# Seven block products instead of eight for chunk 7's second MLP product, in a kernel that already does so for chunks 8 to 11

## The chip, the cores and the metric

The kernel runs on one core of a Trainium2 chip. Its time is the device time of one execution in microseconds (us). A core has a matrix engine (TensorE, PE in the profile, with its weight loads as PEld), a vector engine (VectorE, DVE), an activation engine (ScalarE, ACT), a general engine (GpSimd, POOL) and a queue engine (SyncE, SP) that here only issues transfers. Each engine works through its own list of instructions in a fixed order and waits at an instruction until what it needs has been signalled.

## The reference

Four sequences of 768 positions with 8 heads of 64 go through an attention that sees 8 global and 96 local positions with a linear bias. Its output `x` (4 x 768 x 512) goes through a Fourier mixing layer and an MLP:

```
X = fft(fft(x, axis=1), axis=2)
u = x + real(X)
un = (u - mean(u)) / sqrt(var(u) + 1e-6)
out = u + max(un @ w_ch1, 0) @ w_ch2        # 512 -> 2048 -> 512
```

## The kernel before

**Stages.** The four batches b = 0..3 go through attention, then a two-stage Fourier transform by matrix products, then the MLP. The transform's first stage is in `y_unit` (matmuls at L979 into PSUM tiles `py`, four groups per batch, from sums `eA`, `ww` that VectorE makes at L832 to L859 and L936 to L953). The `py` groups are copied to `zy` on ACT (L994) or VectorE (L996), and POOL makes mirrored copies of them: `ww` (four copies, L1027) and `rev` (L1014 to L1016). The second stage is in `u_unit` (sixteen matmuls at L1059 into `pu`, one call for each pair of residues). VectorE adds the attention output to it (L1078, two instructions with a sum over the row, then L1082), which gives `u`; ACT and VectorE scale it to `un` (L1109, L1111), one half each.

**Chunks.** A chunk c is 256 rows of the MLP, two tiles t = 0, 1 of 128 rows; each batch has three, so c = 0..11, and batch 3 makes chunks 9, 10 and 11. From chunk 6 on `un` is transposed by a DMA that SP issues (L1133) into `unT`. The first product is eight units `ph(c, j)`, j = 0..7, each eight matmuls of 128x256 (L1180), evacuated with a relu to `hT` by ACT (L1186) or VectorE (L1187). ACT also squares `un` for the variance (L1118) once `unT` has landed, and POOL makes the reciprocal deviation (L1125, L1126).

**Second product, plain form (chunks 0 to 7).** `pg_unit` works in parts: for each tile t four parts of four matmuls of 128x512 (L1204), in one PSUM bank, 32 matmuls for the chunk. VectorE adds the scaled result to `u` (L1213), once for each tile, and SP stores the tile (L1218).

**Second product, seven-product form (chunks 8 to 11).** `CS = 8` selects it. The hidden dimension is cut into halves and the 512 output columns into halves, so the chunk's product is a 2x2 by 2x2 block product, and Winograd's scheme makes it from seven block products instead of eight. Each block product is eight matmuls of 128x256 (L1285). The sums that it needs of the weights, `w2_sums`, are made once by VectorE (L1239 to L1242, into the tiles `ex`, when the last attention is done). The sums of each chunk's blocks are four VectorE instructions in `s_sums`: s1 (L1258), s3 (L1261, in place in `hT`), s2 (L1264) and s4 (L1267); s1, s2, s4 go round four buffers in the mask tile `mk`. `pg_units` issues the products as P1 (tile `pgA`), P4 and P5 (`pgD`), P6 (`pgA` again), P3 and P2 (`pgD` again), P7 (`pgA` again). VectorE evacuates them at L1303 with five instructions: 256 columns after P1, 512 after P4 and P5, 256 after P6, 512 after P3 and P2, 512 after P7. The stores are at L1385. `pgA` and `pgD` take the two PSUM banks of the ring `pg`, the ones that the plain form uses too. The seven parts wait for each other: P6 for P1's evacuation (one bank), P3 and P2 for that of P4 and P5, P7 for that of P6.

**Order.** While the program is built, a planner (class `Plan`) decides the order of each engine's list. It keeps a model clock for each engine, takes the work that its costs say can start first, and looks up to ten units ahead in the Fourier and attention streams; the `ph` and `pg` streams are taken strictly in order, each from its head. Its costs are constants in the code, and a few loads have fixed landing times (`LAND`). So a changed unit changes the order of all that comes after it.

Of the kernel before, what the change touches and what calls it, by code (L numbers as in the profile page):

```python
# [181 lines left out]
def mm_us(n, k=1):  # L182
    return k * max(n / 2400.0 + 0.0025, 0.029)


def act(n):
    return 0.06 + n / 1200.0


def dve(n):  # L190
    return 0.085 + n / 960.0
# [11 lines left out]
def kernel(  # L203
# [68 lines left out]
    gb = np.zeros((64, 1))  # L272
# [15 lines left out]
    pl = Plan()  # L288
# [9 lines left out]
    def bank(tag, name, dtype=FP32):  # L298
        if tag in ("C", "D"):
            return early["pool"].tile([P, 2, 512 if dtype == FP32 else 1024], dtype, tag=tag, name=name, bufs=1)  # L300
        if tag == "xx":
            return ps.tile([P, 2, 512 if dtype == FP32 else 1024], dtype, tag=f"{tag}{tag.k}", name=name, bufs=1)
        if "late" not in early:
            early["ctx"].__exit__(None, None, None)
            early["late"] = ctx.enter_context(tc.tile_pool(name="psl", bufs=1, space=bass.MemoryType.PSUM))
        return early["late"].tile([P, 512], FP32, tag=f"{tag}{tag.k}", name=name, bufs=1)
# [5 lines left out]
    def free(tag, i):  # L312
        i -= NBUF[tag]
        return [("free", tag, i)] if i >= 0 else []

    def buf(tag, i, shape, dtype, users):
        pl.users(("free", tag, i), users)
        return wk.tile(shape, dtype, tag=f"{tag}_{i % NBUF[tag]}", name=f"{tag}_{i}", bufs=1)
# [183 lines left out]
    def BANKS(b):  # L502
        return ("xx", "C", "D") if b < 2 else ("xx",)

    def CD(b, ring):
        if b == 1 and ring in ("C", "D"):
            pl.left[("CD",)][0] += 1
            return [("CD",)]
        return [("CD",)] if b == 0 else []

    def RA(b):
        return 2 if b else 0
# [190 lines left out]
    def glob(b, halves):  # L703

        ns = [HP * b + 2 * half + i for half in halves for i in range(2)]
        needs = [("qkT", n) for n in ns] + [("kG", n, s) for n in ns for s in range(2)]

        def run(start, ring):
            pg = bank(ring, f"pgl_{b}_{halves[0]}")
            for half in halves:  # L710
                for i in range(2):
                    hp = 2 * half + i
                    if b >= FB:
                        for x in range(2):
                            nc.tensor.matmul(pg[32 * half:32 * half + 32, 0, x * 256:(x + 1) * 256].rearrange("p (a t m) -> p a t m", a=2, t=2),
                                             kG[b % 2][:, hp, :],
                                             TT[HP * b + hp][:, 0].rearrange("p (i t a m) -> p i a t m", t=2, a=2, m=64)[:, x + 1],
                                             start=(i == 0), stop=(i == 1), tile_position=(0, 32 * half), skip_group_check=True)
                        continue
                    nc.tensor.matmul(pg[32 * half:32 * half + 32, 0, :], kG[b % 2][:, hp, :],  # L720
                                     TT[HP * b + hp][:, 0, 256:S], start=(i == 0), stop=(i == 1),
                                     tile_position=(0, 32 * half))
            e = pl.pe(mm_us(512, 2 * len(halves)), start, True)
            for half in halves:
                pl.tok[("gldone", b, half)] = e
            for n in ns:
                pl.used(("free", "qkT", n), e)
            rows = slice(32 * halves[0], 32 * halves[-1] + 32)

            def ex():  # L730
                if ("free", "eg", b) not in pl.left:
                    pl.users(("free", "eg", b), 8)
                A(EG[rows], pg[rows, 0, :], AF.Exp, gb_sb[rows], 0.125)
            pl.later([("ACT", act(512), ex)], free("eg", b), e, [("eg", b, half) for half in halves], CD(b, ring), ring=ring, rank=RA(b))
        ATT.append((needs, BANKS(b), run))

    X = {}
# [432 lines left out]
    def ph_unit(c, jp):  # L1170
        needs = [("unT", c), ("w1", jp // 2)] + (free("hT", 4 + c) if jp == 0 else []) + [("CD",)]

        def run(start, ring):
            if jp == 0:
                HT[c] = buf("hT", 4 + c, [P, NJ, CH], FP16, 2 if c < CS else 1)
            ph = bank(ring, f"ph_{c}_{jp}")
# [45 lines left out]

    NK = NJ // 2
    HC = Dm // 2
    CS = 8
    SX = {}

    def W2T(i):
# [16 lines left out]
    def s_sums(c):  # L1245
# [5 lines left out]
        def new(i):  # L1251
            k = 3 * (c - CS) + i
            pl.users(("free", "sx", k), 2 if i < 2 else 1)
            SX[c, i] = mk.rearrange("p h n -> p (h n)")[:, (k % 4) * NK * P:(k % 4 + 1) * NK * P].rearrange("p (k n) -> p k n", n=P)
            return SX[c, i]
# [14 lines left out]
        def sfree(i):  # L1270
            k = 3 * (c - CS) + i - 4
            return [("free", "sx", k)] if k >= 0 else []
        pl.later([("DVE", us, s1)], hs + sfree(0), 0.0, [("s", c, 1)], rank=1)
        pl.later([("DVE", us, s2)], [("s", c, 1)] + sfree(1), 0.0, [("s", c, 2)], [("free", "sx", 3 * (c - CS))], rank=1)
        pl.later([("DVE", us, s4)], [("s", c, 2)] + sfree(2), 0.0, [("s", c, 4)], [("free", "sx", 3 * (c - CS) + 1)], rank=1)
        pl.later([("DVE", us, s3)], [("s", c, 1)], 0.0, [("s", c, 3)], rank=1)

    def pg_units(c):
# [23 lines left out]
        def stt(o, x, t, acc):  # L1302
            V.scalar_tensor_tensor(o, x, r(t), acc, op0=ALU.mult, op1=ALU.add)  # L1303
# [9 lines left out]
        def p45(start, ring):  # L1313
# [4 lines left out]
            e = pl.pe(2 * one_us, start)  # L1318
            pl.used(("free", "sx", 3 * (c - CS)), e)
            pl.later([("DVE", dve(Dm), lambda: stt(u(1), D_, 1, u(1)))],  # L1320
# [273 lines left out]
```

## Time and profile before

| | |
|---|---|
| four runs before | 264.11, 265.17, 265.50, 267.08 us; median 265.34 |
| the profiled execution | 264.11 us, its span 262.3 us |
| TensorE matmuls | 244.4 us busy, 93% of the span |
| VectorE | 176.6 us, 67% |
| ScalarE | 146.4 us, 56% |
| GpSimd | 67.9 us, 26% |
| TensorE clock granted | 1.00 |

A row's start is given from the span's start. The durations of matmuls overlap, since they are pipelined, so what a unit costs TensorE is read from the starts of consecutive units: eight matmuls of 128x256 start 0.87 us before the next unit, four of 128x512 start 0.86 us before it. The same holds for VectorE, whose rows overlap a little: a 128x512 addition at L1213 lasts 0.74 us and the next instruction starts 0.66 us after it.

### The profile page before, as it was taken

The page shows a single profiled execution, that of the slowest core. Times are in us where ns is not written, and L with a number is a line of the kernel's source. Part 1 is how long each engine was busy: PE and PEld are TensorE (multiplying, and loading weights), DVE is VectorE, ACT ScalarE, POOL GpSimd, SP SyncE. Part 2 cuts the span into 40 slices and gives each one's busy share as a digit, 9 for nine tenths or more (in the row PEclk, how much of TensorE's full clock was granted, in tenths as well). Part 3 has the DMA queues.
Part 4 walks back from the last instruction along what each step waited for, and adds up shares of the span by engine and source line. Part 5 has one row for each costly group of instructions (what it writes and reads, how often), then busy time and mean ns, then how long its engine had stood idle before and what let it go on. Part 6 is the DMA issues. An engine that isn't in the chain of part 4 may idle for free.

```text
span 262.3 us, 7311 instructions
## 1 busy us (share of the span) xinstructions
PE 244.4 (93%) x3080; PEld 178.7 (68%) x3080; DVE 176.6 (67%) x360; ACT 146.4 (56%) x249; POOL 67.9 (26%) x133
## 2 busy tenths in 40 slices
PE   8787668599999999999999999999999999999994
PEld 2565555487856876774685565679677568888883
DVE  4568997842599746661398968777998734644463
ACT  1468879776476577963861445995346165433300
POOL 1445398652030515123110523011001320010000
PEclk9999999999999999999999999999999999999999
DMA  7999969999599993995999895502071330310222
GB/s 216 296 292 302 308 173 248 217 215 207 117 260 241 250 195 96 222 223 102 237 157 207 240 234 115 140 0 42 17 202 65 82 84 36 82 42 2 80 81 82
DMA packets 76386, 42.02 MB, mean 160 GB/s; under 512 B 33474, under 2 KB 72514, under 8 KB 76354
## 3 DMA queue, kind: packets, MB, share of 16 engines
q1 hardware_dynamic: 69298, 32.65, 55.7%
q0 software_dynamic: 4224, 4.19, 9.5%
q10 hardware_dynamic: 2832, 4.72, 6.5%
q8 instruction: 24, 0.39, 0.6%
q14 instruction: 8, 0.07, 0.1%
HBM read 31.59 MB, written 9.44 MB: 156 GB/s over the span
## 4 chain that ended last, share of the span: by engine, by line
PE 79%; ACT 6%; DVE 4%; POOL 4%; DMA 3%; issue 2%; SPq 1%; POOLq 0%; ACTq 0%; DVEq 0%
PE ph L1180 31%; PE pg L1204 21%; PE pgD L1285 5%; PE pgA L1285 4%; PE pav L768 4%; PE py L979 3%; PE pu L1059 3%; DMA u<-in_v_dram 3%; PE sc L630 2%; ACT ex L657 2%; POOL ww L1027 2%; PE pav L757 2%; SPq L399 1%; DVE qkT L586 1%; DVE x L788 1%
## 5 line engine op out<-in xcount | busy, mean ns | idle before, releaser
L1180 PE MATMUL ph<-unT,w 128*128 128x256 f16 x768 | 93.3, 273 | 0.0
L1180 PEld LDWEIGHTS <-w 128*128 128x128 f16 x768 | 72.8, 98 | 13.6 <-issue 2.6
L1186 ACT ACTIVATE hT<-ph 128x512 f16<-128x512 f32 x78 | 46.1, 597 | 45.1 <-PE ph L1180 43.3
L1204 PE MATMUL pg<-w,hT 128*128 128x512 f16 x256 | 60.0, 379 | 0.0
L1204 PEld LDWEIGHTS <-hT 128*128 128x128 f16 x256 | 24.3, 98 | 24.6 <-issue 0.7
L657 ACT ACTIVATE ex<-sc 128x992 f16<-128x992 f32 (+2 forms) x24 | 20.6, 928 | 7.4 <-PE sc L633 7.3
L654 ACT ACTIVATE er<-sc 128x992 f16<-128x992 f32 (+2 forms) x24 | 21.6, 928 | 4.5 <-PE sc L630 4.3
L1213 DVE SCALAR_TENSOR_TENSOR u<-pg,sm,u 128x512 f32<-128x512 f32 x16 | 11.9, 745 | 12.9 <-PE pg L1204 12.8
L669 DVE TENSOR_TENSOR ex<-er,mk 128x992 f16<-128x992 f16 (+2 forms) x24 | 15.4, 643 | 7.1 <-ACT er L654 6.8
L1027 POOL COPY ww<-zy 128x512 f16<-128x512 f16 x16 | 10.0, 650 | 29.9 <-PE py L979 29.9
L1125 POOL TENSOR_SCALAR sm<-sm 128x2 f32<-128x2 f32 x12 | 2.5, 209 | 56.9 <-ACT un L1118 54.6
L768 PEld LDWEIGHTS <-ex 128*128 128x128 f16 x352 | 15.1, 97 | 2.7 <-issue 1.8
L768 PE MATMUL pav<-v,ex 128*128 128x65 f16 x352 | 16.3, 193 | 0.5 <-ACT ex L657 0.3
L1118 ACT ACTIVATE un<-un 128x512 f16<-128x512 f16 x24 | 14.9, 627 | 3.0 <-DMA unT<-un 2.5
L1187 DVE TENSOR_SCALAR hT<-ph 128x512 f16<-128x512 f32 x18 | 12.4, 687 | 6.1 <-PE ph L1180 5.9
L403 ACT ACTIVATE qk<-qs 128x768 f16<-128x768 f32 x11 | 9.2, 841 | 12.1 <-DMA out_dram<-u 7.2
L1109 ACT ACTIVATE un<-u,sm 128x512 f16<-128x512 f32 x16 | 11.2, 718 | 8.2 <-DVE sm L1082 8.2
L1078 DVE SCALAR_TENSOR_TENSOR u<-pu,xr 128x512 f32<-128x512 f32 x18 | 11.7, 686 | 4.0 <-PE pu L1059 3.8
L493 POOL CAST v<-qs 128x768 f16<-128x768 f32 x8 | 6.6, 829 | 27.4 <-DMA qs<-in_v_dram 27.4
L1285 PEld LDWEIGHTS <-hT 128*128 128x128 f16 x128 | 12.5, 98 | 1.6
L788 DVE TENSOR_TENSOR x<-pav,rc 128x512 f16<-128x512 f32 (+1 forms) x21 | 12.9, 615 | 0.7
L536 POOL COPY kG<-qkT 64x8 f16<-64x8 f16 x32 | 9.8, 307 | 13.3 <-DVE qkT L586 10.1
(122 smaller groups left out, 377.3 us busy)
## 6 DMA issues: line engine op xcount, KB each, us to landing
out_dram<-u SPq DMA_DIRECT2D x23, 256.0 KB, 2.4
w<-in_moe_w_ch_dram POOLq DMA_DIRECT2D x8, 512.0 KB, 19.3
qs<-in_q_dram SPq DMA_DIRECT2D x9, 384.0 KB, 5.6
qs<-in_k_dram SPq DMA_DIRECT2D x9, 384.0 KB, 5.3
qs<-in_v_dram SPq DMA_DIRECT2D x16, 192.0 KB, 5.2
xr<-xd ACTq DMA_DIRECT2D x3, 768.0 KB, 5.7
u<-in_v_dram SPq DMA_DIRECT2D x5, 384.0 KB, 7.2
w<-in_q_dram SPq DMA_DIRECT2D x4, 384.0 KB, 6.3
```

The source lines that it names most:

```text
L654: A(mine(), cut(pa), AF.Exp, 0.0, 0.125)
L657: A(cut(expst[hp][:, :, g * 512:g * 512 + (384 if g == 2 else 512)]), cut(pa), AF.Exp, 0.0, 0.125)
L669: VT(o, mine(), m, op=ALU.mult)
L768: nc.tensor.matmul(po[:, jj, hh * 65:(hh + 1) * 65], lhsT, v16[b % 2][:, i, h, 0:65], start=(jp == 0 and a == 0), stop=(a == len(ops) - 1) ...
L788: VT(X[b][:, 2 * jp:2 * jp + 2, first * Dh:(first + nh) * Dh].rearrange("p j (h d) -> p j h d", d=Dh), pv[:, :, :, 0:Dh], rc.to_broadcast( ...
L1027: nc.gpsimd.tensor_copy(rev[:, n], T[("y", b)][:, n, :, :, ::-1])
L1118: A(x, x, AF.Square, accum_out=MV[c][:, a, 2:3])
L1180: nc.tensor.matmul(ph[:, a * CH:(a + 1) * CH].rearrange("p (x m) -> p x m", x=2), W1[0][:, d, jb * P:(jb + 1) * P], UNT[c][:, :, d, :], st ...
L1186: pl.later([("ACT", act(512), lambda: A(dst, ph, AF.Relu)), ("DVE", dve(512), lambda: V.tensor_scalar_max(dst, ph, 0.0))], [], e, [("h", c ...
L1187: ("DVE", dve(512), lambda: V.tensor_scalar_max(dst, ph, 0.0))],
L1204: nc.tensor.matmul(pg, HT[c][:, jb, t * P:(t + 1) * P], W2[0][:, jb, :], start=(jb == 0), stop=(jb == NJ - 1))
L1285: nc.tensor.matmul(o, lhs(j), rhs(j), start=(first and j == 0), stop=(j == NK - 1), skip_group_check=True)
```

## The change

`CS` goes from 8 to 7, so chunk 7 takes the seven-product form too. The second line changed adds a need to the global keys' exponential (L733), that the small bias tile `gb` has been loaded; the order up to chunk 6 is the same with it as without.

```diff
@@ glob
-            pl.later([("ACT", act(512), ex)], free("eg", b), e, [("eg", b, half) for half in halves], CD(b, ring), ring=ring, rank=RA(b))
+            pl.later([("ACT", act(512), ex)], free("eg", b) + [("c", "gb")], e, [("eg", b, half) for half in halves], CD(b, ring), ring=ring, rank=RA(b))
@@
     NK = NJ // 2
     HC = Dm // 2
-    CS = 8
+    CS = 7
     SX = {}
```

For chunk 7, 32 matmuls of 128x512 become 56 of 128x256; two VectorE additions of 512 columns become five (three of 512, two of 256 columns); VectorE gets four sums of 1024 elements per partition. The first difference in any list lies in the first product of chunk 8. TensorE's list from there, with `6.t` for the parts of chunk 6's tile 1:

```
before: 6.t part 0 | ph 8.3 8.4 | 6.t part 1 | ph 8.5 8.6 | py0 py3 | ph 8.7 | 6.t part 2 |
        py1 py2 | 6.t part 3 | pu 9 | 7 part 0 | pu 11 | 7 part 1 | pu 10 | 7 parts 2 to 6 |
        ph 9.0 9.1 | 7 part 7 | ph 9.2 9.3 | 8 P1 | ph 9.4 9.5 | 8 P4 P5 | ph 9.6 9.7 | 8 P6 |
        ph 10.0 10.1 | 8 P3 P2 | ...
        ph 11.6 11.7 | 10 all seven | 11 all seven
after:  6.t part 0 | ph 8.3 8.4 | 6.t part 1 | ph 8.5 8.6 | 6.t part 2 | ph 8.7 | 6.t part 3 |
        py0 py3 | 7 P1 P4 P5 | py1 py2 | 7 P6 | pu 9 | 7 P3 P2 | pu 10 | pu 11 | 7 P7 |
        8 P1 P4 P5 P6 | ph 9.0 9.1 | 8 P3 P2 | ph 9.2 9.3 | 8 P7 | ph 9.4 9.5 | 9 P1 | ...
        ph 11.6 11.7 | 10 P3 P2 P7 | 11 all seven
```

VectorE's list in the same place (F is the transform's first sums, L851 to L859, G the second, L936 to L953):

```
before: F, G | py3 copy | relu 8.7 | sums s1 s2 s3 s4 of 8 | 6.t add | pu 9 add, un | pu 10 add, un |
        7 add | 7 add | ...
after:  s1 of 7 | first of F | s2 of 7 | relu 8.3 | s3 of 7 | rest of F | s4 of 7 | G | 6.t add |
        s1 of 8 | 7 P1 add | s3 of 8 | 7 P4 P5 add | s2 of 8 | py2 copy (1024) | 7 P6 add | s4 of 8 |
        pu 9 add | 7 P3 P2 add | un 9 | pu 10 add | 7 P7 add | un 10 | 8 P1 add | ...
```

ACT copies py0, py3 and py1 instead of py0, py1 and py2. On SP the store of chunk 7's tile 0 now stands ahead of the transpose for chunk 9, and that of its tile 1 ahead of the transpose for chunk 10; before, both stood behind the two transposes.

## The prediction

> **What bounds the kernel now.** I read the busy time by stretch first, then TensorE's timeline over the stage that changes, then VectorE's and the transposes. By stretches (columns: length, then busy us and instructions of TensorE's matmuls, weight loads, VectorE, ScalarE, GpSimd, then the clock and DMA share):
>
> ```profile
> 192.15:211.87 19.72, 19.34 (x158) 13.24 (x156) 15.68 (x35) 8.24 (x13) 3.73 (x7) 1.00 0.35 101
> 211.87:244.17 32.30, 32.30 (x293) 28.58 (x292) 14.59 (x26) 15.37 (x31) 2.64 (x6) 1.00 0.18 55
> ```
>
> The new order begins near 192.15 and chunk 9's first product near 211.87. TensorE is full in both stretches; VectorE is at 80% in the first, where it also makes batch 3's transform, and at 45% in the second. So matmul time counts one for one, as long as VectorE and the transposes keep up. TensorE's timeline:
>
> ```profile
> 201.73 1.03 PE L1204 MATMUL pg<-w,hT 128*128 128x512 f16 x4
> 202.59 1.06 PE L1059 MATMUL pu<-t,zy 128*128 128x128 f16 x16
> 203.48 1.03 PE L1204 MATMUL pg<-w,hT 128*128 128x512 f16 x4
> 204.35 0.28 PE L1059 MATMUL pu<-t,ww 128*128 128x128 f16 x2
> 205.00 0.96 PE L1059 MATMUL pu<-t,ww 128*128 128x128 f16 x14 [0.38 <-POOL ww L1027]
> ...
> 207.55 4.48 PE L1204 MATMUL pg<-w,hT 128*128 128x512 f16 x20
> 211.87 1.91 PE L1180 MATMUL ph<-unT,w 128*128 128x256 f16 x16
> ...
> 222.34 1.04 PE L1285 MATMUL pgA<-ex,mk 128*128 128x256 f16 x8
> 223.21 1.91 PE L1180 MATMUL ph<-unT,w 128*128 128x256 f16 x16
> ```
>
> The starts give the unit prices: 20 wide matmuls take 211.87 - 207.55 = 4.32, so 0.216 each; eight narrow ones take 223.21 - 222.34 = 0.87 (0.8735 over many). The only stall is 0.54, before 205.00 (204.35 + 0.11 for two matmuls = 204.46), for the mirrored copies.
>
> **The product itself.** 32 x 0.216 = 6.91 goes; 56 x 0.1092 = 6.11 comes: **-0.80 us**. Chunks 8 to 11 already run at this narrow price, and a weight load lasts 98 ns against 109 ns from one narrow matmul to the next, so the loads stay hidden, narrowly.
>
> The Trainium skill, "TensorE: Matmul & The Clock Gate", section "Back-to-back issue gap", speaks against the change: in streams of a weight load and a matmul it gives about 131 ns for each 512-column matmul and 81 ns for a 128-column one. An estimate between these for 256 columns is 98 ns, and by it the change would cost 56 x 0.098 - 32 x 0.131 = +1.3 us. The rows here, 216 and 109 ns, contradict it and follow that section's formula for isolated matmuls instead, so the measurement decides.
>
> **VectorE's added work.** A sum of 1024 elements takes 0.61 to the next start (0.73 where it needs the one before it):
>
> ```profile
> 201.06 0.69 DVE L1264 TENSOR_TENSOR mk<-mk,hT 128x1024 f16<-128x1024 f16 x1
> 201.67 0.68 DVE L1261 TENSOR_TENSOR hT<-hT 128x1024 f16<-128x1024 f16 x1
> 202.27 1.10 DVE L1267 TENSOR_TENSOR mk<-hT,mk 128x1024 f16<-128x1024 f16 x1
> 203.29 0.74 DVE L1213 SCALAR_TENSOR_TENSOR u<-pg,sm,u 128x512 f32<-128x512 f32 x1
> ```
>
> Four sums: 2.44. Evacuations: 3 x 0.66 + 2 x 0.40 instead of 2 x 0.66: +1.46. Together +3.9 on VectorE, none of it on TensorE; it is hidden if nothing that TensorE needs comes late. So I walk the new order with these intervals.
>
> *First sums.* All four of chunk 7's sums and the relu of 8.3 now stand ahead of G. F and G as a block move by 4 x 0.61 + 0.61 = 3.05. In the trace the sums that py0 needs end about 196.5, now near 199.5. TensorE does 6.t's last two parts and ph 8.7 first: 197.37 + 2 x 0.865 + 0.873 = 199.97. Margin 0.47, no stall; without it each further 0.1 on VectorE costs 0.1. The relu of 8.3 ends by 195.1, ph 8.5 starts at 195.62. G ends at 201.2, py1 starts at 203.75.
>
> *7 P1 to pu 9.* py0 and py3 end at 201.06, P1 at 201.93; P4 needs the bank that the 6.t addition frees at 202.0 (stall 0.07), P5 ends at 203.75, py2 at 205.28, P6 at 206.15, pu 9 at 207.04. P6 needs VectorE's addition of P1, done by 202.9.
>
> *Mirrors.* In the trace POOL starts them 0.29 after py2, takes 2.88 for `ww` and 0.84 for `rev`, so 205.57 to 209.3. 7 P3 and P2 end at 208.79; pu 10 then needs `rev` and waits some 0.15 after two matmuls; pu 11 ends at 210.72. The old stall of 0.54 goes in exchange: **-0.4**.
>
> *Back-pressure.* VectorE copies py2 (1024 wide, about 1.15) from 205.5, adds P6, makes s4 of chunk 8, then pu 9's 1.33 and 0.20, P3 and P2, `un`, pu 10, and only then P7, whose bank 8 P4 needs. I get P7's addition ending at 212.5, 8 P4 starting at 212.55 instead of 212.47 (+0.1), 8 P6 ending at 215.2.
>
> In the fence above L1267 took 1.10 instead of 0.68 while POOL copied (202.02 to 204.95); s3, which only its last 0.3 shares with the copies, stayed at 0.68. In the new order s4 of chunk 8 lies wholly beside the copies too. So all that follows on VectorE may come 0.42 later, and 8 P4 with it. The ends are 0.1 and 0.55; I take **+0.55**, since L1267's is the same instruction beside the same copies. 8 P6 then ends at 215.6.
>
> The Trainium skill, "SBUF — State Buffer", section "Who interferes with whom", says that a VectorE instruction with two SBUF inputs and a GpSimd one that reads SBUF exclude each other for a whole instruction, whichever began first. By that rule s4 waits for a whole copy (0.72) at worst, and the sum would be 0.3 worse than with the 0.42.
>
> *The transpose.* Before, `un` of chunk 9 was done at 206.2 and TensorE reached it at 211.87:
>
> ```profile
> 205.48 0.72 ACT L1109 ACTIVATE un<-u,sm 128x512 f16<-128x512 f32 x1 [2.27 <-DVE sm L1082]
> 210.91 0.63 ACT L1118 ACTIVATE un<-un 128x512 f16<-128x512 f16 x1 [0.83 <-DMA unT<-un]
> ```
>
> The view of chunk transposes gives:
>
> ```profile
> DMA to landing us min/median/max: 3.0/3.1/4.8
> ```
>
> The transposes started at 206.2 and 222.6 took 4.7 and 4.8, those at 164.7 and 210.1 took 3.1. Now `un` is done at 210.25 to 210.75 (VectorE: pu 9 at 207.65 or 208.1, statistics 1.53, P3 and P2 0.67, half of `un` 0.45). The store ahead of it on SP waits for P3 and P2's addition, just earlier, and takes 0.33 to issue. So the transpose starts at 210.4 to 210.9, lands at 213.5 at best and 215.2 to 215.7 at worst. TensorE wants it at 215.2, or 215.6 if VectorE is late, which moves both. I take no stall. The cover is 0 to 2 us; once gone, each us is a us.
>
> *Behind it.* ACT's scaling of chunk 11 waits for VectorE's pu 11 addition (216.2 to 217.7, after chunk 7's second store, issued about 213 and landed in 2.0 to 2.4), and behind it stand chunk 10's squares and relu 9.2. They end by 219.9, relu 9.2 is due at 220.1; hidden. Chunk 10's transpose starts near 213.4 and is wanted after 222. From 8 P3 on 48 units of 0.8735 remain: 41.93. The tail keeps about 0.4 of waits between blocks: before, three of 0.14; now 0.28 where 11 P1 waits for the bank of 10 P3 and P2, whose addition stands behind two sums, and 0.14 where 11 P3 waits. So TensorE ends at 215.6 + 41.9 + 0.4 = 257.9 (257.5 from the other end), against 258.54 before: **-0.6**, at best -1.0. (By terms: -0.80, -0.4 at the mirrors, +0.55, +0.07, the same tail.) After it come the same addition and store.
>
> The profiled execution took 264.11 (span 262.3), the fastest of four; the median is 265.34. -0.6 on the execution gives 263.5, on the median **264.7**, which I forecast. 1% (2.65 us) is about what a measurement here can tell from no change; the forecast lies inside it.
>
> **Rivals.** *Gain eaten on VectorE.* py0 comes 0.2 late and the mirrored copies 0.4 (four of them took 2.27 at 155.67 and 2.94 at 202.02, beside the sums): -0.6 + 0.6 = 0, **265.3**. For it: VectorE has hardly a gap from 190 to 213 in the walk. Against: 0.47 of margin at py0.
>
> *Slower: chunk 9's transpose comes late.* Place: ph 9.0. Chunk 7's store (256 KB) goes out 0.4 before the transpose; if the transpose waits until it has landed, that is 210.0 + 2.0 to 2.4 = 212.3, and with 4.8 it lands at 217.1, or 217.5 with VectorE late, 1.9 after TensorE is ready: -0.6 + 1.9 = +1.3, **266.6**. It decides from a landing 0.6 after that point, at 216.2. For it: nothing is left on TensorE's list to fill with, where before 20 wide matmuls stood. Against: the transpose's 3.1 at 164.7 came 1.9 after a store, with a transpose between them.
>
> *No saving by itself:* if narrow matmuls with chunk 7's operands ran at more than 123 ns, the product would gain nothing: -0.6 + 0.8, **265.5**. Every narrow row speaks against it.
>
> **How the numbers follow.** Forecast (gain of 0.3 to 1.0, 264.3 to 265.0) 0.60; eaten on VectorE 0.20; late transpose 0.16; no saving 0.04. The range reaches from the forecast's best, 264.3, less 0.7 for scatter (the lowest run stood 1.2 under the median), 263.6, to the late transpose with a little of VectorE's on top, 266.8. Chances: faster by over 1% 0.03, only by scatter; within 1% 0.90; slower by over 1% 0.07, the late transpose with more than the 1.9.
>
> **What would show it.** Chunk 7's seven products at 0.87 each; no wait of `py` on VectorE; one short wait of `pu` on `rev`; a wait at 8 P4 of 0.1 to 0.55; no idle before ph 9.0; TensorE's last unit near 257.7. I am wrong if TensorE idles before ph 9.0, at py0, or if a relu comes late after chunk 11's scaling on ACT.

## The result, and the profile after

| | before | changed |
|---|---|---|
| median of the timed runs | 265.27 us (79 runs) | 263.97 us (53 runs) |
| ratio, 95% interval | | 0.9954 [0.9941, 0.9968] |
| the profiled execution, its span | 264.11, 262.3 us | 263.23, 261.4 us |

The changed kernel is faster by 1.2 us (0.8 to 1.6). The forecast was 0.6 us faster, 264.7 us. So the time lies inside the range and within 1% of before, with the forecast's sign, and the gain is twice the one forecast. It is also more than the 0.3 to 1.0 that the forecast allowed itself: 263.97 lies below its 264.3 to 265.0, in the part of the range that was added for scatter, so that the range held is partly luck. The ratio compares the means of the executions without the few that were slower as a whole, so it is not quite the ratio of the two medians.

The busy times on the changed kernel's page, section 1 (busy us, share of the span, instructions):

```profile
PE 243.2 (93%) x3104; PEld 181.0 (69%) x3104; DVE 178.7 (68%) x366; ACT 146.5 (56%) x250; POOL 66.8 (26%) x133
```

TensorE lost 1.2 of its 244.4 us and VectorE gained 2.1, less than the 3.9 of added work, in part because one relu went over to ACT (17 at L1187 where there were 18). The changed kernel by stretches, with the columns of the prediction's first fence; the first runs from the new order's start to chunk 9's first product:

```profile
192.45:215.31 22.86, 22.86 (x219) 19.11 (x217) 20.90 (x45) 8.30 (x14) 3.63 (x8) 1.00 0.39 114
215.31:250.00 34.69, 34.69 (x320) 31.11 (x318) 15.14 (x28) 16.78 (x32) 2.54 (x6) 1.00 0.14 41
```

TensorE shows no idle time in the first stretch, where before it lacked 0.38 of 19.72. VectorE is at 20.90 of 22.86, 91% where it was 80%, and back at 44% in the second. TensorE's timeline of the changed kernel (start, duration, instruction, count, idle time before and its releaser):

```profile
199.41 1.03 PE L1204 MATMUL pg<-w,hT 128*128 128x512 f16 x4
200.27 1.26 PE L979 MATMUL py<-t,ww 128*128 128x256 f16 x10
201.36 1.04 PE L1285 MATMUL pgA<-w,hT 128*128 128x256 f16 x8
202.24 1.04 PE L1285 MATMUL pgD<-ex,hT 128*128 128x256 f16 x8
...
209.02 0.28 PE L1059 MATMUL pu<-t,zy 128*128 128x128 f16 x2
209.13 0.28 PE L1059 MATMUL pu<-t,rev 128*128 128x128 f16 x2
...
211.68 1.04 PE L1285 MATMUL pgA<-w,hT 128*128 128x256 f16 x8
212.69 1.03 PE L1285 MATMUL pgD<-ex,hT 128*128 128x256 f16 x8
...
214.43 1.04 PE L1285 MATMUL pgA<-ex,mk 128*128 128x256 f16 x8
215.31 0.93 PE L1180 MATMUL ph<-unT,w 128*128 128x256 f16 x7
```

Chunk 7's blocks follow each other in 0.87 (201.36, 202.24), and py0 comes straight behind the last wide part (199.41 + 0.86 = 200.27). No row carries a bracket with idle time: a wait under about 0.17 hides in the modelled ends and shows only in the starts. There is one, before 8 P4: 211.68 + 0.87 = 212.55, and it starts at 212.69, 0.14 late. Chunk 9's first product follows 8 P6 at once (214.43 + 0.87 = 215.30). The tail of the same view holds the two others:

```profile
250.24 1.04 PE L1285 MATMUL pgA<-ex,hT 128*128 128x256 f16 x8
251.46 1.03 PE L1285 MATMUL pgA<-w,hT 128*128 128x256 f16 x8 [0.18 <-DVE u L1303]
...
254.07 1.04 PE L1285 MATMUL pgA<-ex,mk 128*128 128x256 f16 x8
255.08 1.03 PE L1285 MATMUL pgD<-w,mk 128*128 128x256 f16 x8
```

11 P1 waits 0.35 (251.46 - 250.24 - 0.87) and 11 P3 waits 0.14. TensorE's last unit is issued by 257.69, where it was 258.54.

**Where the time went.** From the start of chunk 6's tile 1 (192.15 before, 192.45 after; all that differs lies behind it) to the end of the last unit TensorE took 66.39 us before and takes 65.24, so **-1.15**, which agrees with the 1.2 of the clock. (The execution's own difference is only 0.88 because the changed one reached this point 0.30 later.) The terms:

| term of the prediction | forecast | measured |
|---|---|---|
| the product of chunk 7 | -0.80 | -0.80 |
| the mirrors (0.54 before pu 11, then pu 10) | -0.4 (0.15 stays) | -0.54 (nothing stays) |
| stall at 7 P4 | +0.07 | 0 |
| back-pressure, 8 P4 | +0.55 | +0.14 |
| tail | 0 | +0.08 (0.49 instead of 0.41) |
| sum | -0.6 | -1.12 |

The rest of the document asks whether these terms are causes or a lucky sum, and why two were mis-sized. Below, "TensorE's stretch" is always this one, from that start to the end of the last unit. It tells 0.1 us (the changed kernel gave the same to a hundredth in each of three traces), which the clock cannot: its intervals reach 0.7 to 0.9 us to either side in the experiments. All kernels below have the second changed line too, and the kernel before has not. With chunk 7 in the plain form three of them differ from it by -0.42, +0.61 and -0.56 us on the clock and by -0.40, +0.71 and -0.56 in TensorE's stretch, so that line by itself costs or saves nothing that shows.

### The profile page after: what moved, and what is told of

Read it like the earlier page. It is cut to its first block, busy times and chain, and to the rows that moved or that the text cites. A ratio compares the mean times of both kernels' runs of the same rounds, so it can differ in the third digit from the quotient of the medians.

```text
span 261.4 us, 7364 instructions
## 1 busy us (share of the span) xinstructions
PE 243.2 (93%) x3104; PEld 181.0 (69%) x3104; DVE 178.7 (68%) x366; ACT 146.5 (56%) x250; POOL 66.8 (26%) x133
## 4 chain that ended last, share of the span: by engine, by line
PE 66%; DMA 17%; DVE 7%; ACT 4%; issue 2%; SPq 2%; POOL 1%; POOLq 0%; ACTq 0%
PE ph L1180 25%; PE pg L1204 15%; DMA w<-in_moe_w_ch_dram 9%; PE pgD L1285 6%; PE pgA L1285 5%; PE pu L1059 3%; PE py L979 3%; DMA u<-in_v_dram 3%; PE sc L630 2%; PE pav L768 2%; DMA qs<-in_k_dram 2%; DVE x L788 2%; DMA xr<-xd 2%; SPq L399 2%; DMA xd<-hT 2%
## 5 line engine op out<-in xcount | busy, mean ns | idle before, releaser
L1186 ACT ACTIVATE hT<-ph 128x512 f16<-128x512 f32 x79 | 46.8, 598 | 48.6 <-PE ph L1180 48.5
L1204 PE MATMUL pg<-w,hT 128*128 128x512 f16 x224 | 52.5, 379 | 0.0
L1213 DVE SCALAR_TENSOR_TENSOR u<-pg,sm,u 128x512 f32<-128x512 f32 x14 | 10.4, 744 | 8.7 <-PE pg L1204 8.7
L1187 DVE TENSOR_SCALAR hT<-ph 128x512 f16<-128x512 f32 x17 | 11.7, 687 | 5.8 <-PE ph L1180 5.7
L1303 DVE SCALAR_TENSOR_TENSOR u<-pgD,sm,u 128x512 f32<-128x512 f32 (+1 forms) x11 | 7.7, 701 | 10.0 <-PE pgD L1285 9.8
```

Of the source, the lines that this page charges most:

```text
L1186: pl.later([("ACT", act(512), lambda: A(dst, ph, AF.Relu)), ("DVE", dve(512), lambda: V.tensor_scalar_max(dst, ph, 0.0))], [], e, [("h", c ...
L1187: ("DVE", dve(512), lambda: V.tensor_scalar_max(dst, ph, 0.0))],
L1204: nc.tensor.matmul(pg, HT[c][:, jb, t * P:(t + 1) * P], W2[0][:, jb, :], start=(jb == 0), stop=(jb == NJ - 1))
```

## The experiments

**The changed kernel again.** Theory A is the sum of terms: the product's 0.80 and the mirrors' wait are both real. Theory B is that the product gains nothing by itself and that the whole gain is the new order's, the wait that went. The run repeats the changed kernel on another chip.

> The changed kernel again, as the yardstick for the other runs on this chip. Theory A (the gain is a sum of separate terms on TensorE: -0.80 for chunk 7's cheaper product, -0.54 for the wait before pu 11 that goes, +0.14 and +0.08 for new waits at 8 P4 and in the tail): -1.1 us, a ratio near 0.996. Theory B (narrow products save nothing here, the gain is only the wait that went and the rest is scatter): -0.4 to -0.5, a ratio near 0.998.

264.83 against 266.11, ratio 0.9957 [0.9928, 0.9985]. TensorE's stretch is 65.24 again, with the waits 0.13, 0.35 and 0.13 in the same places. The gain exceeds B's 0.4 in the trace, and the terms are the same to a hundredth.

**Only pu 10 and pu 11 exchanged, chunk 7 in the plain form.** In batch 3 pu 11 has to stand behind pu 10, as it does in the changed kernel.

```diff
+            pl.tok[("puo", b, pr)] = e
-        MIX.append((needs + [("c", "t2")], BANKS(b), run))
+        MIX.append((needs + [("c", "t2")] + ([("puo", b, 1)] if b == B - 1 and pr == 2 else []), BANKS(b), run))
-    CS = 7
+    CS = 8
```

> CS stays 8, so chunk 7 is in the plain form, but batch 3's second transform is held to the order pu 9, pu 10, pu 11, as in the changed kernel: the one part of the new order that took the 0.54 us wait away. Theory A: TensorE does 7 part 0 and 1 between pu 9 and pu 10 (1.73 us), so pu 10 waits for the mirrored copies only 0.1 to 0.2 us: -0.4 us, ratio 0.9985. Theory B: nearly all of the changed kernel's gain, -1 us, ratio 0.996.

265.32, ratio 0.9984 [0.9951, 1.0017]. TensorE's stretch is 65.99, 0.40 less than before: the 0.54 goes and pu 10 waits 0.15. That is the prediction's term at the mirrors, alone and to the hundredth. It leaves 0.75 for the product and its waits, so B falls. But in the changed kernel pu 10 did not wait, while the four copies took as long here as before (2.94, then 2.93), so something else also differs.

**The seven-product form from chunk 9 on.** One chunk fewer in it than before.

```diff
-    CS = 7
+    CS = 9
```

> CS = 9: chunk 8 goes back to the plain form, in the stretch where TensorE is full and VectorE has room, so the price of the form stands alone. Order and waits before chunk 9's first product are those of the kernel before (the 0.54 wait stays). Theory A: 56 x 0.1092 becomes 32 x 0.216, +0.80 us against the kernel before, ratio 1.003. Theory B: no change.

266.14, ratio 1.0023 [0.9988, 1.0058]; TensorE's stretch is 67.10, 0.71 more than before, close to the +0.80 of the product. The agreement is partly an accident. The wait of 0.54 before pu 11 is gone, though the order there is the old one, and a new wait of 0.49 has come at 10 P4: 0.80 - 0.54 + 0.49 = 0.75. The mirrored copies and that wait in this kernel's timeline:

```profile
203.29 2.28 POOL L1027 COPY ww<-zy 128x512 f16<-128x512 f16 x4 [18.13 <-PE py L979]
...
247.44 1.04 PE L1285 MATMUL pgA<-w,hT 128*128 128x256 f16 x8
248.80 1.03 PE L1285 MATMUL pgD<-ex,hT 128*128 128x256 f16 x8 [0.33 <-DVE u L1303]
```

All four copies took 0.61 each and 2.28 together. Before, they took 2.93, and single rows of that kernel's timeline show which two:

```profile
202.02 0.81 POOL L1027 COPY ww<-zy 128x512 f16<-128x512 f16 x1 [18.14 <-PE py L979]
202.77 1.07 POOL L1027 COPY ww<-zy 128x512 f16<-128x512 f16 x1
203.79 0.61 POOL L1027 COPY ww<-zy 128x512 f16<-128x512 f16 x1
```

The fourth took 0.61 as well. The first two lie beside s3 (from 201.67) and s4 (from 202.27) of chunk 8, sums that the kernel with `CS = 9` doesn't make. That gave theory C: the old stall was no price of the mirrors, but was made by VectorE's own sums. They held the copies up by 0.20 and 0.46, together 0.66, and TensorE waited 0.54.

**Chunk 8's sums held back, chunk 7 in the plain form.** The test of C: the order of `pu` stays the old one (9, 11, 10), and s2, s3 and s4 of chunk 8 may start only when pu 9 has been added.

```diff
-    CS = 7
+    CS = 8
-        pl.later([("DVE", us, s2)], [("s", c, 1)] + sfree(1), ...
+        pl.later([("DVE", us, s2)], [("s", c, 1)] + sfree(1) + ([("u", 9, 0)] if c == 8 else []), ...
```

(The same addition stands in the needs of s3.)

> CS = 8 and the pu units in the old order 9, 11, 10, but chunk 8's sums s2, s3, s4 are held back on VectorE until pu 9 has been added, so that none of them lies beside POOL's four mirrored copies. Theory C (a VectorE sum with both inputs in SBUF and a POOL copy exclude each other; the old wait of 0.54 before pu 11 came from two such sums holding POOL's copies up by 0.2 and 0.5): the four copies start 0.55 apart, the wait before pu 11 is gone, -0.5 us against the kernel before, ratio 0.998. Rival (the copies are simply that long, and the order of the pu units decides): the wait of 0.54 stays, no change.

264.9 against 265.58, ratio 0.9979 [0.9949, 1.0009]. TensorE's stretch is 65.83, 0.56 less than before. This kernel's timeline:

```profile
203.39 2.27 POOL L1027 COPY ww<-zy 128x512 f16<-128x512 f16 x4 [18.14 <-PE py L979]
...
204.86 1.03 PE L1204 MATMUL pg<-w,hT 128*128 128x512 f16 x4
205.72 1.06 PE L1059 MATMUL pu<-t,ww 128*128 128x128 f16 x16
```

The copies are unhindered, pu 11 (205.72) follows part 0 of chunk 7 (204.86 + 0.86) at once, and nothing else moved. C holds. So nearly half of the change's gain can be had without it: beside this kernel the change is worth 65.83 - 65.24 = 0.59, the product's 0.80 less the waits it adds.

**The four copies as one instruction.** In the changed kernel, batch 3's four mirrored copies become one of 2048 columns. If sum and copy shut each other out for whole instructions, s4 of chunk 8 now waits for the end of the long one; if copies only slow a sum by a fixed share, it does not. The change, without its indices:

```diff
-            nc.gpsimd.tensor_copy(rev[:, n], T[("y", b)][:, n, :, :, ::-1])
+            if b < B - 1:
+                nc.gpsimd.tensor_copy(rev[:, n], T[("y", b)][:, n, :, :, ::-1])
+            elif n == 3:
+                nc.gpsimd.tensor_copy(...all four at once...)
```

> The changed kernel, with batch 3's four mirrored copies of 512 columns made as one POOL instruction of 2048. Theory C: the sum s4 of chunk 8, which meets this copy about 1.4 us after its start, waits for its end, 0.7 us, where it now waits 0.2 for the end of a short one; everything behind it on VectorE comes 0.5 later, and 8 P4 waits 0.6 to 0.7 instead of 0.14: +0.5 us against the changed kernel, ratio about 0.998 against the kernel before. Rival (a sum beside a copy is slowed by a fixed 0.2 to 0.4, whatever the copy's length): 8 P4 waits 0.14 to 0.3, no change against the changed kernel.

265.08, ratio 0.9973 [0.9938, 1.0007]. TensorE's stretch is 65.72, 0.48 more than the changed kernel's. The timeline of this kernel (its lines are four further down: L1271 is s4, L1307 the additions, L1289 the blocks):

```profile
207.77 1.89 POOL L1030 COPY ww<-zy 128x2048 f16<-128x2048 f16 x1 [21.96 <-ACT zy L994]
...
208.48 0.47 DVE L1307 SCALAR_TENSOR_TENSOR u<-pgA,sm,u 128x256 f32<-128x256 f32 x1
208.87 1.33 DVE L1271 TENSOR_TENSOR mk<-hT,mk 128x1024 f16<-128x1024 f16 x1
210.13 0.68 DVE L1082 SCALAR_TENSOR_TENSOR u<-pu,xr 128x512 f32<-128x512 f32 x1
...
213.31 1.04 PE L1289 MATMUL pgA<-w,hT 128*128 128x256 f16 x8
214.80 1.03 PE L1289 MATMUL pgD<-ex,hT 128*128 128x256 f16 x8 [0.45 <-DVE u L1307]
```

The sum takes 1.26 to the next start instead of 0.60, so it waited 0.66, until the copy was through near 209.6; 8 P4 then waits 0.62. The addition at 208.48, which reads one operand from PSUM, lies beside the same copy and lasts 0.47 as ever. So a copy shuts out the sums, which have both inputs in SBUF, for the rest of that copy, and lets the additions pass. That it is the place of the inputs that decides, and not the kind of the instruction, no run separates. The Trainium skill, "SBUF — State Buffer", section "Who interferes with whom", calls this "an exclusive lock" between VectorE and GpSimd, and the runs agree with that.

**The seven-product form from chunk 6 on.** How far does the gain go?

```diff
-    CS = 7
+    CS = 6
```

> CS = 6: chunk 6 takes the seven products too. If only TensorE counted, -0.8 us more than the changed kernel (ratio 0.993). But VectorE gets another 3.9 us between 176 and 212 us, where the changed kernel leaves it hardly any gap, and the first sums of the weights are only done at about 187 us. Theory A, with VectorE as the bound: the py and pu units and the seven products of chunks 6 and 7 wait for VectorE, 1 to 3 us in all, so between the changed kernel's time and 2 us over the kernel before. Theory B: the time of the changed kernel, since the form saves nothing.

266.96, ratio 1.0009 [0.9978, 1.004]: all that chunk 7 gained is lost again. Chunk 6 lies ahead of TensorE's stretch, so here the time is taken from a score product that is the same in both (172.18 before, 174.35 here): 86.38 to the last unit's end, where before took 86.36 and the changed kernel's stretch is 1.15 shorter. Its timeline, and its stretches of 5 us (busy us and counts as above):

```profile
194.81 1.03 PE L1180 MATMUL ph<-unT,w 128*128 128x256 f16 x8 [0.29 <-ACT hT L1186]
...
203.45 1.30 PE L979 MATMUL py<-t,ww 128*128 128x256 f16 x10 [0.43 <-DVE ww L938]
...
208.03 1.03 PE L1285 MATMUL pgD<-w,mk 128*128 128x256 f16 x8 [0.66 <-DVE u L1303]
```

```profile
195.00:200.00 5.00, 5.00 (x48) 4.48 (x47) 5.00 (x12) 1.44 (x3) 0.00 (x0) 1.00 0.67 142
200.00:205.00 5.00, 4.54 (x40) 3.58 (x39) 4.97 (x10) 0.00 (x0) 0.00 (x0) 1.00 0.49 191
205.00:210.00 5.00, 4.34 (x41) 3.73 (x40) 4.93 (x11) 1.51 (x2) 0.00 (x0) 1.00 0.15 56
```

VectorE is full and TensorE waits for it: 0.60 and 0.83 at the second and third row shown, and 0.19 for an addition at 201.98. The first row shown waited 0.45 for a relu on ACT; that one stood behind the issue of two transfers of `x` (L807, 192.84 to 194.11), which go out when VectorE has made `x`, at 192.81. With 0.49 in the tail this is 2.56 of waits, 0.63 in the changed kernel, so +1.93 against the second product's -0.80, which is +1.13. The rival "gain eaten on VectorE" is a real mechanism; it decides one chunk further on.

**Two more sums on VectorE.** How much of VectorE's time was left? In the changed kernel two extra sums of 1024 elements stand ahead of G; their result goes to an unused buffer and changes nothing.

```diff
         def s3():
             VT(block(1, 0), block(0, 0), block(1, 0), op=ALU.subtract)
+            if c == 7:
+                for _ in range(2):
+                    VT(mk...[5th buffer], SX[c, 0], SX[c, 0], op=ALU.add)
```

> The changed kernel, with two more VectorE sums of 1024 elements ahead of G (their result is not used), 1.2 us on VectorE. py0 started 0.5 after its inputs were ready, so it should now wait 0.7; and since VectorE has no gap until 205, the bank that 7 P4 needs, freed by the 6.t addition, comes late too, another 0.4 to 0.5: about +1.2 us against the changed kernel, ratio about 1.000 against the kernel before. If VectorE had room here, no change against the changed kernel.

266.41, ratio 1.0016 [0.9988, 1.0043]. TensorE's stretch is 66.56, 1.32 more, for 1.33 of extra work. TensorE's timeline of this kernel:

```profile
201.94 1.03 PE L1204 MATMUL pg<-w,hT 128*128 128x512 f16 x4
203.16 1.30 PE L979 MATMUL py<-t,ww 128*128 128x256 f16 x10 [0.20 <-DVE ww L938]
204.29 1.04 PE L1288 MATMUL pgA<-w,hT 128*128 128x256 f16 x8
206.09 1.03 PE L1288 MATMUL pgD<-ex,hT 128*128 128x256 f16 x8 [0.76 <-DVE u L1213]
```

py0 waits 0.35 and 7 P4 waits 0.93. So the margin at py0 was 1.0: its first matmuls need only the sums of L938, done at 199.24 in the changed kernel and wanted at 200.27. The prediction's 0.47 was too small. At 7 P4, which waits for the last plain addition (L1213) behind G, there was no margin left, and the two waits together take the whole 1.33.

**The transpose made late.** In the changed kernel six transfers of 8 KB, of the tile just stored and to scratch, go out on SP ahead of chunk 9's transpose.

```diff
                 nc.sync.dma_start(out[b]...[:, rs[t], :], u(t))
+                if c == 7 and t == 0:
+                    for x in range(6):
+                        nc.sync.dma_start(dup[x], u(t)[:, 16 * x:16 * x + 16])
```

> The changed kernel, with six small extra transfers (8 KB each) on SP between chunk 7's first store and chunk 9's transpose. It tests the cover that the prediction gave this transpose: it landed at 213.7, TensorE came at 215.3, so 1.6 us. Six issues of 0.35 to 0.5 us hold it back by 2.1 to 3 us, so TensorE idles 0.5 to 1.4 us before ph 9.0 (up to 3 if the landing takes 4.7 instead of 3.0), and the time grows by the same. If the transpose does not matter here at all, nothing changes.

266.22, ratio 1.0036 [1.0006, 1.0065]. TensorE's stretch is 66.59, 1.35 more. This kernel's timeline:

```profile
212.99 2.84 SPq L1389 DMA_DIRECT2D dup<-u  x6
215.99 1.23 SPq L1133 DMA_TRANSPOSE unT<-un  x1
...
219.10 1.91 PE L1180 MATMUL ph<-unT,w 128*128 128x256 f16 x16 [1.19 <-DMA unT<-un]
```

The transpose starts some 2.9 later than it would have, and lands 3.0 after its start; 1.35 of the 2.9 is a wait, so 1.5 was cover. That is the prediction's cover of 0 to 2 us, and the rival "late transpose" has the place it was given.

**Two more stores ahead of the transpose.** The rival's mechanism was that the transpose waits until chunk 7's store has landed. Two more stores of 256 KB, of the same tile to scratch, would then hold it up by more. There is one execution of this kernel.

```diff
+                if c == 7 and t == 0:
+                    for x in range(2):
+                        nc.sync.dma_start(dup[x], u(t))
```

> The changed kernel, with chunk 7's first store made three times (the two extra ones to a scratch tensor), all ahead of chunk 9's transpose on SP: 768 KB in flight instead of 256 KB when the transpose is issued. If the transpose waits until stores ahead of it have landed (the prediction's rival), it lands 2.4 us or more later than its issue lets it, at 217 or later, and TensorE idles 1 us or more before ph 9.0. If it only waits for its issue, two more issues of 0.35 to 0.5 hold it back by 0.7 to 1.0, it lands 3.0 after its start, within the cover of 1.6, and TensorE idles not at all.

263.93 in the one execution; TensorE's stretch is 65.24, as in the changed kernel, with no idle time before ph 9.0. The transpose was issued at 212.49, which is 1.48 after the first store, against 0.51 in the changed kernel; the 0.97 more is what the two more take to issue. The three stores landed at 213.05, 213.74 and 214.62. The transpose's own landing is not on record, but ACT, idle until then, starts its squares at 216.01, 3.5 after the transpose's start, where the changed kernel has 3.1. So it landed some 0.4 later than usual, which the expectation had not; had it waited for the last store, its usual 3.0 from there would end at 217.6, and TensorE, which came at 216.15, would have idled. The transpose waits for the issue of what stands ahead of it, not for its landing.

**The tail's sums held back.** 11 P1 waits 0.35 because s1 and s2 of chunk 11 stand on VectorE ahead of the addition of 10 P3 and P2, whose bank 11 P1 needs. First form: s2 and s3 of chunk 11 start only after the first tile of chunk 10 is done. Second form: only after the second.

```diff
-        pl.later([("DVE", us, s2)], [("s", c, 1)] + sfree(1), ...
+        pl.later([("DVE", us, s2)], [("s", c, 1)] + sfree(1) + ([("ob", c - 1, 0)] if c == NP * B - 1 else []), ...
```

(The second has `("ob", c - 1, 1)`; s3 gets the same need.)

> The changed kernel, with chunk 11's sums s2, s3, s4 held until the addition of 10 P3 and P2, which stood behind s1 and s2 and freed the bank for 11 P1 late: the one wait left in the tail that the order makes (0.35). The walk: 11 P1 waits 0.05 to 0.15 instead of 0.35, P6 still finds s2 ready: -0.2 us against the changed kernel, ratio 0.9945 to 0.9950 against the kernel before. If the tail's waits are only moved (11 P6 waits for s2 instead), no change.

> As the last tail run, but chunk 11's s2, s3, s4 are held until the addition of 10 P7 as well, which frees the other bank, for 11 P4. 11 P1 waits 0.14, 11 P4 0.0 to 0.1, P6 finds s2 ready; 0.35 + 0.14 of waits become 0.14 + 0.14 to 0.24: -0.1 to -0.2 us against the changed kernel in the trace, too little for the clock times to tell. If it only moves the wait again (11 P6 or P3), no change.

The first failed: 264.96, ratio 0.9972 [0.994, 1.0004], TensorE's stretch 65.42, 0.18 more than the changed kernel's. 11 P1 waits 0.14 now, but s2 stands ahead of the next addition instead and 11 P4 waits 0.39. The second: 264.78 against 265.64, ratio 0.9933 [0.9899, 0.9968], TensorE's stretch 65.13. TensorE's timeline of the second:

```profile
250.54 1.04 PE L1285 MATMUL pgA<-ex,hT 128*128 128x256 f16 x8
251.55 1.03 PE L1285 MATMUL pgA<-w,hT 128*128 128x256 f16 x8
...
254.17 1.04 PE L1285 MATMUL pgA<-ex,mk 128*128 128x256 f16 x8
255.28 1.03 PE L1285 MATMUL pgD<-w,mk 128*128 128x256 f16 x8
```

11 P1 waits 0.14 and 11 P3 0.24, a tenth less in all. Beside it the changed kernel ran once more:

> The changed kernel beside the run above, as its yardstick: 65.2 us on TensorE from 6.t part 0 to the last matmul, ratio 0.9945 to 0.997 against the kernel before.

264.3, ratio 0.9942 [0.9909, 0.9975], TensorE's stretch 65.24. The clock doesn't tell the two apart; that the second form beats the changed kernel is shown by a tenth in one trace and by no more.

## Why the prediction was right, and where it was off

**The product itself** is right. Chunk 7's seven blocks take 0.873 each, and the kernels with `CS` 9 and 7 differ by two products and their waits: 2 x 0.80 + 0.91 - 0.63 = 1.88, measured 67.10 - 65.24 = 1.86. The clock's 0.8 to 1.6 us of gain leaves no room for the +1.3 that the prediction worked out from the Trainium skill's figures.

**First sums.** No wait, as forecast. The margin was mis-sized, 1.0 and not 0.47, because py0 was taken to need all of its sums at once. The two extra sums show it.

**7 P1 to pu 9.** The stall of 0.07 at 7 P4 was not there (201.36 + 0.87 = 202.23, started 202.24), but there was nothing to spare: each further 0.1 on VectorE cost 0.1.

**Mirrors**, the first mis-sized term: -0.4 forecast, -0.54 measured. The forecast took the four copies to be as long as before. With 205.57 + 2.88, and 0.51 for the first two instructions of `rev`, the first half of `rev` is done at 208.96, and pu 10's third matmul is due at 208.79 + 0.11 = 208.90: a short wait, put at 0.15. GpSimd's rows of the changed kernel:

```profile
205.80 2.73 POOL L1027 COPY ww<-zy 128x512 f16<-128x512 f16 x4 [21.62 <-PE py L979]
208.60 0.39 POOL L1015 COPY rev<-zy 128x254 f16<-128x254 f16 x1
```

The copies took 2.73 and not 2.94, because s4 of chunk 8 still meets them but s3 no longer does, and s3 was worth 0.20. So `rev`'s first half is done at 208.99 and wanted at 209.13. With chunk 7 in the plain form and pu 10 ahead of pu 11, pu 10's third matmul was due as soon after the start of the copies (3.30, here 3.33), but both sums lay beside them, and there the 0.15 appeared. The deeper error is in the reading of before. The prediction's first rival quotes four copies at 2.27 and, beside the sums, at 2.94, and its back-pressure step has L1267 at 1.10 beside the copies; but the sum of terms took the longer copies as given and the 0.54 as the price of the mirrors. It was the price of two sums placed beside them: holding the sums back removed it without the change. In the new order one of the two sums is there still; the wait goes mostly because pu 10 stands ahead of pu 11, which alone gave 0.40, and the rest of it, by the rows, because the copies are 0.20 shorter.

**Back-pressure**, the term that failed: +0.55 forecast, +0.14 measured. The 0.42 added to s4 was taken as a fixed price for running beside copies. What a sum pays is the rest of the copy in flight when it comes up. VectorE's and GpSimd's rows of the changed kernel:

```profile
206.85 0.47 DVE L1303 SCALAR_TENSOR_TENSOR u<-pgA,sm,u 128x256 f32<-128x256 f32 x1
206.90 0.61 POOL L1027 COPY ww<-zy 128x512 f16<-128x512 f16 x1
207.24 0.81 DVE L1267 TENSOR_TENSOR mk<-hT,mk 128x1024 f16<-128x1024 f16 x1
207.46 1.07 POOL L1027 COPY ww<-zy 128x512 f16<-128x512 f16 x1
207.98 0.68 DVE L1078 SCALAR_TENSOR_TENSOR u<-pu,xr 128x512 f32<-128x512 f32 x1
...
211.89 0.75 DVE L1303 SCALAR_TENSOR_TENSOR u<-pgA,sm,u 128x512 f32<-128x512 f32 x1
```

s4's turn comes when the addition ahead of it ends, at 206.85 + 0.47 = 207.32, and the third copy lets it in when the fourth starts, at 207.46: 0.14, which is what it lost (0.74 to the next start instead of 0.60). In the same way the 0.42 of before is 202.77 - 202.35. In turn s4 holds the fourth copy, 1.07 instead of 0.61. The 0.14 did not reach 8 P4. The addition of chunk 7's P7 starts at 211.89, 0.31 after that block's last matmul started, and the same 0.31 stands in the tail, where VectorE is idle ahead of it. VectorE came just in time: that addition follows the row before it after 0.11, where 0.08 is usual, so 0.03 was to spare. So the 0.14 at 8 P4 is the bare hand-over of a bank from a block to the addition and on to the next block but one, the same 0.14 as in the tail before the change. The low end of the prediction's bounds, 0.1, was near; it took the high one. With the long copy the loss was 0.52 more, 0.66, and 8 P4 waited 0.48 more, 0.62, so the path from s4 to 8 P4 is the one that the prediction drew, and only the size on it was off. By the same count even a loss of 0.42 would have made 8 P4 wait some 0.4 and not 0.55 (an estimate: 0.14 + 0.42 - 0.14 - 0.03).

**The transpose** is right. SP's and ACT's rows of the changed kernel's timeline:

```profile
210.16 0.33 SPq L1385 DMA_DIRECT2D out_dram<-u  x1
210.67 1.29 SPq L1133 DMA_TRANSPOSE unT<-un  x1
...
213.79 0.63 ACT L1118 ACTIVATE un<-un 128x512 f16<-128x512 f16 x1 [1.03 <-DMA unT<-un]
```

It starts at 210.67 (forecast 210.4 to 210.9), lands 3.0 later, and TensorE comes for it at 215.31: a cover of 1.6. A landing of 4.7, as this same transpose took before the change, or of 4.8, as chunk 11's did, would have come at 215.3 to 215.5, a wait of up to 0.2. With chunk 7 in the plain form chunk 9's transpose took 3.7 to 4.7 in all four traces; with chunk 7 in the seven-product form it took 3.0 to 3.1 in all but the one with three stores ahead of it (some 3.4). What decides between them stays open; the 1.6 lies in the forecast's 0 to 2 without having been derived.

**Behind it.** ACT's chain was not late (relu 9.2 starts at 219.87, right behind its product). The tail's waits are 0.49, where the prediction had the same "about 0.4" on both sides: 0.35 at 11 P1 instead of 0.28.

So the total was off by the two waits nearly alone: 0.41 of the 0.55 at 8 P4 was not there, and 0.14 more went at the mirrors. The other terms held to a tenth. The waits were put in the right places, and both errors are of size; that the other two small ones, -0.07 at 7 P4 and +0.08 in the tail, cancel is chance.

## What to carry to other kernels

When a row is longer beside another engine's work, look at that engine's rows too: the cost of the meeting is paid on both sides, and the dearer half may already stand in the profile under another name, here as TensorE's wait for the mirrors. The price is the rest of the instruction in flight, so it depends on the moment and on the length of the other's instructions; a figure from one meeting is not a rate, and here four short copies were kinder to a sum than one long one. A change that moves work from an engine that is full to one that has room is worth its own price until the second is full in that very stretch: at 91% of VectorE chunk 7 gained 0.6 to 1.2 us, near 100% chunk 6 gave it all back.

## What the runs showed of the hardware

- A VectorE sum with both inputs in SBUF and a GpSimd copy between SBUF tiles exclude each other. The sum lost 0.14, 0.42 and 0.66 us according to what was left of the copy (the longest beside one copy of 1.89), and then held the next copy by some 0.46 (1.07 instead of 0.61). An addition with one operand in PSUM lies beside the same copies at its usual 0.47.
- The hand-over of a PSUM bank between blocks of 0.87 that leave one block between them costs TensorE 0.13 to 0.14, also when VectorE is idle.
- Transfers ahead of a transpose on SP delay its start by their issue, some 0.48 each for six of 8 KB and as much for two of 256 KB. Three stores of 256 KB ahead of it did not hold it until they had landed, but it landed some 0.4 later after its start than the usual 3.0.
